# First products two units ahead of second products in the unpinned half of an attention and two-mixer kernel

## The chip, the cores and the metric

The kernel runs on one core of one Trainium2 chip. The metric is the device time of one execution in microseconds (us). The kernel before took 886.29 us, the median of 3 runs (883.88 to 888.55).

## The reference, cut to what matters

Three blocks follow one another on 4 sequences of 576 tokens and 512 features. The first is an attention (a coarse one over means of 4 tokens, plus a local one over 7 neighbours). The second and third are mixers; all weights are float32.

```
x  = attention(q, k, v)                                   # (4, 576, 512)
xn = (x - mean) / sqrt(var + 1e-6) * g_ln
x  = x + max(xn @ w_ch1, 0) @ w_ch2                       # w_ch1 512x2048, w_ch2 2048x512
h  = max(x^T @ w_tok1, 0) @ w_tok2                        # over tokens: 576x256, 256x576
u  = x + h^T
out = u + max(u @ w_ch1', 0) @ w_ch2'                     # w_ch1' 512x1536, w_ch2' 1536x512
```

## The kernel before, in words

The 2304 tokens are 18 tiles of 128, two tiles to a chunk: 9 chunks for the first channel mixer (chunks 0 to 8) and 9 for the second (chunks 9 to 17). A **unit** is one chunk with 128 hidden features. A chunk has 16 units in the first mixer and 12 in the second, 252 units in all (`seq`, lines 858 to 860). Chunk 7 begins with unit 112, chunk 9 with unit 144, and units 144 to 155 are chunk 9.

A unit has four steps.

- `g1` (line 868), the first products: 12 matmuls of 256 columns into a PSUM bank `h`. Each float32 operand is kept as two fp32r halves, high and low, and three of the four combinations are multiplied (`PASSES`: high-high, high-low, low-high), for each of four slices of the 512 features.
- `relu` (line 882): ScalarE (ACT) writes the high half of the hidden tile `ht` from `h`.
- `low` (line 886): VectorE (DVE) writes the low half of `ht` from `h` and the high half.
- `g2` (line 892), the second products: 6 matmuls of 512 columns from `ht` and the second weight into two accumulators `acc`. Four of the six need the high half of `ht` alone, the other two its low half.

Two buffers each hold `h`, `ht` and `acc` (`bufs=2`, lines 208, 210 and 211).

Up to unit 111 the order of everything is a table written out by hand (`STEPS`), pinned with `manual_schedule`. **Behind unit 112** the kernel only traces its instructions in a loop over units (lines 1205 to 1214, in the diff below): first products of a later unit, the background steps that `put` has hung on this unit (`mid`), second products of this unit, a chunk's end, and more background steps (`bg`). The Tile framework then makes each engine's order from this by priority and its own model of time. So an engine's order can differ from the traced one, and the place of a background step moves when the loop changes.

The background steps that the prediction touches:

- **Weights of the second mixer**: 24 pieces of 512 KB. The queue of SyncE (SP) issues a load into a staging buffer `st` (line 298, two buffers). Three DVE steps turn a piece from float64 into float32 (`cv`, lines 257, 262, 267). ACT writes the high half (`w`, line 272) and DVE the low half (line 275).
- **Token tiles**: each of the 4 sequences has five tiles for the token mixer. `xs_load` (line 961) loads a tile from DRAM into `xr`, of which there is one buffer (lines 962 and 970, or 968 for the fifth tile, in two pieces). `xs_split` (line 973): ACT writes the high half of `xs` (line 976), GpSimd (POOL) the low half (line 977). `tok1` (line 983): six matmuls (line 992) into banks `k`. After a sequence's fifth tile `tok_relu` (line 997) makes `r` on ACT and DVE, and `tok2` (line 1012) multiplies it by the second token weight (line 1023).
- **Turning of `u`** for the next chunk: `xt_turn`, 32 small DMAs a chunk on the SP queue (line 818).

```
    def xs_load(b, n):
        t = tok["pool"].tile([128, DM], F32, tag="xr", name="xr", bufs=1)
...
    def xs_split(b, n):
        r = xs[b, n]
        t = tok["pool"].tile([128, 2, DM], F32R, tag="xs", name="xs", bufs=2)
        nc.scalar.activation(out=t[:, 0], in_=r, func=ACTF.Copy)
        nc.gpsimd.tensor_tensor(out=t[:, 1], in0=r, in1=f32(t[:, 0]), op=ALU.subtract)
```

Of the kernel before, what the change touches and what calls it, by code (L numbers as in the profile page):

```python
# [170 lines left out]
UNITS = 112  # L171
# [26 lines left out]
def block_kernel(ctx: ExitStack, tc: tile.TileContext, qk, vw, vh, vg, g_ln, wa, t1, t2, wb, band, near, lv, edge, out):  # L198
# [693 lines left out]
    def g2(i):  # L892
        c, m = seq[i]
        w = wunit(c, m)
        t = hT.pop(i)
        last = m == nunits(c) - 1
        for j in range(CT):
            if m == 0:
                acc[c, j] = psg("k" if c == 1 else "acc")
            for n, (a, e) in enumerate(PASSES):  # L900
                nc.tensor.matmul(  # L901
                    out=acc[c, j], lhsT=t[:, a, j * 128:(j + 1) * 128], rhs=w[:, 1, e, :],
                    start=(m == 0 and n == 0), stop=(last and n == 2),
                )
# [16 lines left out]
    def chunk_end(i):  # L921
        c, m = seq[i]
        if m == nunits(c) - 1:
            with tc.high_priority(offset=HP2):
                for j in range(CT):
                    evac(i, j)
                    store(i, j)
# [103 lines left out]
    NSEQ = len(seq)  # L1031
# [171 lines left out]
    put_tok(3, base[NCH + 4])  # L1203

    for i in range(UNITS, NSEQ):
        if i + 1 < NSEQ:
            for f in (g1, relu, low):
                f(i + 1)
        for f in mid[i]:
            f()  # L1210
        g2(i)
        chunk_end(i)
        for f in bg[i]:
            f()
# [121 lines left out]
```

## Time and profile before

| | |
|---|---|
| median of 3 runs (range) | 886.29 us (883.88 to 888.55) |
| profiled execution: its own time | 886.56 us |
| profiled execution: span of the trace | 884.8 us |
| mean granted TensorE clock | 0.998 |
| TensorE (PE) busy | 863.8 us, 98% |
| weight loads (PEld) busy | 766.3 us, 87% |
| DVE, ACT, POOL busy | 518.4, 251.4 and 193.6 us |

A profile is one execution. Its times count from the start of the span, which is 1.8 us shorter than the execution's own time. Line numbers are those of the kernel before. PE is matmuls; a "releaser" is what ended an engine's wait.

### The profile page before, as it was taken

How to read it: one execution, taken by the hardware profiler on the slowest of the kernel's cores; microseconds unless marked ns; L12 is line 12 of the kernel's file. 1: busy time of each engine (PE TensorE's matmuls, PEld its weight loads, DVE VectorE, ACT ScalarE, POOL GpSimd, SP SyncE). 2: the span in 40 equal slices, each digit the busy share in tenths (PEclk: the TensorE clock that was granted, in tenths of full speed). 3: DMA queues.
4: the chain of work that ended last, by engine and by line, in shares of the span. 5: the costliest groups of instructions: out<-in, count | busy, mean ns of one | idle time of the engine just before them, and what ended most of it. 6: DMA issues, size and time to landing. Idle time of an engine off the chain costs nothing.

```text
span 884.8 us, 16767 instructions
## 1 busy us (share of the span) xinstructions
PE 863.8 (98%) x6418; PEld 766.3 (87%) x6418; DVE 518.4 (59%) x1114; ACT 251.4 (28%) x713; POOL 193.6 (22%) x197
## 2 busy tenths in 40 slices
PE   7999999999999999999999999989999999999998
PEld 6888899887989999989999887879898898999997
DVE  5999999999998776832222779863213232222221
ACT  5665535354322111322111233222121111111111
POOL 7731323566873510111000000110010000000000
PEclk9999999999999999999999999999999999999999
DMA  9747776578662522532111356632222121121100
GB/s 280 193 151 225 225 237 199 148 199 224 168 150 72 139 49 60 175 92 89 36 37 48 107 155 178 193 115 53 52 56 46 29 67 35 17 45 23 31 24 24
DMA packets 126752, 98.39 MB, mean 111 GB/s; under 512 B 78744, under 2 KB 104376, under 8 KB 126672
## 3 DMA queue, kind: packets, MB, share of 16 engines
q1 hardware_dynamic: 126672, 97.31, 39.4%
q8 instruction: 51, 0.84, 0.4%
q14 instruction: 29, 0.24, 0.1%
HBM read 72.87 MB, written 16.53 MB: 101 GB/s over the span
## 4 chain that ended last, share of the span: by engine, by line
PE 66%; DVE 19%; DMA 8%; SPq 3%; issue 2%; POOL 1%; ACT 1%; DVEq 0%; ACTq 0%; POOLq 0%
PE h L875 30%; PE acc L901 27%; DMA xr<-x_scr 3%; DMA st<-in_wb_dram 3%; SPq L818 3%; PE k L901 2%; DVE cv L267 2%; PE g L1023 2%; DVE ht L888 1%; DVE cv L262 1%; DVE lp L718 1%; DVE la L726 1%; DVE cv L257 1%; PE k L992 1%; DMA up_scr<-od 1%
## 5 line engine op out<-in xcount | busy, mean ns | idle before, releaser
L875 PEld LDWEIGHTS h<-xt,w 128*128 128x128 f32 x3024 | 394.2, 191 | 22.9 <-DVE ht L888 2.1
L875 PE MATMUL h<-xt,w 128*128 128x256 f32 x3024 | 404.8, 284 | 1.4 <-DVE ht L888 1.3
L901 PE MATMUL acc<-w,ht 128*128 128x512 f32 x1416 | 367.7, 395 | 3.0 <-DVE ht L888 2.4
L901 PEld LDWEIGHTS acc<-w,ht 128*128 128x128 f32 x1416 | 253.5, 189 | 52.3 <-DVE ht L888 4.6
L888 DVE SCALAR_TENSOR_TENSOR ht<-h,ht 128x256 fp32r<-128x256 f32 x252 | 105.6, 419 | 273.4 <-ACT ht L884 273.0
L884 ACT ACTIVATE ht<-h 128x256 fp32r<-128x256 f32 x252 | 96.7, 384 | 439.0 <-PE h L875 355.8
L977 POOL TENSOR_TENSOR xs<-xr,xs 128x512 fp32r<-128x512 f32 x20 | 26.5, 1323 | 293.3 <-ACT xs L976 293.3
L272 ACT ACTIVATE w<-cv 128x512 fp32r<-128x512 f32 x56 | 35.5, 635 | 66.6 <-DVE cv L267 66.5
L684 POOL TENSOR_TENSOR lp<-lqk 128x576 f32<-128x576 f32 x28 | 40.4, 1444 | 43.2 <-DVE ls L690 31.5
L275 DVE TENSOR_TENSOR w<-cv,w 128x512 fp32r<-128x512 f32 x56 | 42.8, 767 | 4.3 <-ACT w L272 4.1
L267 DVE SCALAR_TENSOR_TENSOR cv<-st,cv 128x512 int32<-128x512 int32 (+4 forms) x63 | 44.2, 703 | 0.4
L655 POOL TENSOR_TENSOR x<-x,et 128x256 f32<-128x256 f32 (+2 forms) x40 | 32.0, 820 | 50.6 <-DMA et<-loc_scr 40.0
L262 DVE SCALAR_TENSOR_TENSOR cv<-st,cv 128x512 int32<-128x512 int32 (+4 forms) x63 | 41.5, 659 | 0.4
L257 DVE TENSOR_SCALAR cv<-st 128x512 int32<-128x512 int32 (+4 forms) x63 | 27.3, 433 | 15.2 <-DMA st<-in_wb_dram 10.5
L455 POOL TENSOR_TENSOR vg<-vg 72x256 f32<-72x256 f32 x39 | 31.4, 806 | 18.3 <-DMA vg<-in_vg_dram 15.3
L992 PE MATMUL k<-xs,t1w 128*128 128x512 f32 (+1 forms) x120 | 32.1, 406 | 2.6 <-ACT xs L976 1.9
L1023 PE MATMUL g<-r,t2w 128*128 128x512 f32 x120 | 34.0, 394 | 0.0
L830 ACT ACTIVATE xt<-xt 128x512 fp32r<-128x512 f32 x30 | 18.9, 631 | 34.6 <-DMA xt<-xc 31.2
L835 DVE TENSOR_TENSOR xt<-xt 128x512 fp32r<-128x512 f32 x30 | 24.1, 803 | 7.3 <-ACT xt L830 7.0
L901 PE MATMUL k<-w,ht 128*128 128x512 f32 x96 | 26.0, 403 | 0.1
L992 PEld LDWEIGHTS k<-xs,t1w 128*128 128x128 f32 (+1 forms) x120 | 19.2, 188 | 7.9 <-ACT xs L976 2.8
L1023 PEld LDWEIGHTS g<-r,t2w 128*128 128x128 f32 x120 | 20.9, 189 | 3.0
(189 smaller groups left out, 656.4 us busy)
## 6 DMA issues: line engine op xcount, KB each, us to landing
st<-in_wa_dram SPq DMA_DIRECT2D x28, 512.0 KB
st<-in_wb_dram SPq DMA_DIRECT2D x24, 512.0 KB
xt<-xc SPq DMA_DIRECT2D x480, 16.0 KB
qk<-in_qk_dram SPq DMA_DIRECT2D x13, 581.0 KB
x_scr<-x SPq DMA_DIRECT2D x18, 256.0 KB
x<-x_scr SPq DMA_DIRECT2D x9, 512.0 KB
out_dram<-x SPq DMA_DIRECT2D x18, 256.0 KB
xr<-x_scr SPq DMA_DIRECT2D x16, 256.0 KB
```

The costliest lines, as they stand in the source:

```text
L257: return nc.vector.tensor_scalar(out=f, in0=h, scalar1=3, scalar2=0x3FFFFFFF, op0=ALU.logical_shift_left, op1=ALU.bitwise_and)
L262: nc.vector.scalar_tensor_tensor(out=f, in0=h, scalar=-0x40000000, in1=f, op0=ALU.bitwise_and, op1=ALU.bitwise_or)
L267: nc.vector.scalar_tensor_tensor(out=f, in0=l, scalar=29, in1=f, op0=ALU.logical_shift_right, op1=ALU.bitwise_or)
L272: nc.scalar.activation(out=hi, in_=f.bitcast(F32), func=ACTF.Copy)
L275: nc.vector.tensor_tensor(out=lo, in0=f.bitcast(F32), in1=f32(hi), op=ALU.subtract)
L684: nc.gpsimd.tensor_tensor(out=t["pr"], in0=t["qk"][:, :VQ], in1=t["qk"][:, VQ + D * o:VQ + D * o + VQ], op=ALU.mult)
L875: nc.tensor.matmul(out=hp[:, :CN], lhsT=w[:, 0, a, kk * 128:(kk + 1) * 128], rhs=xT[c][:, kk, e, :], start=(n == 0), stop=(n == 3 * KD - 1),)
L884: nc.scalar.activation(out=t[:, 0], in_=hps[i][:, :CN], func=ACTF.Relu)
L888: nc.vector.scalar_tensor_tensor(out=t[:, 1], in0=hp[:, :CN], scalar=0.0, in1=f32(t[:, 0]), op0=ALU.max, op1=ALU.subtract)
L901: nc.tensor.matmul(out=acc[c, j], lhsT=t[:, a, j * 128:(j + 1) * 128], rhs=w[:, 1, e, :], start=(m == 0 and n == 0), stop=(last and n == 2),)
L992: nc.tensor.matmul(out=rps[b, m], lhsT=tokw["t1"][rows, a, n, m * 128:(m + 1) * 128], rhs=t[rows, e, :], start=(n == 0 and i == 0), stop=( ...
L1023: nc.tensor.matmul(out=ps, lhsT=tokw["t2"][:, a, m, o:o + 128], rhs=r_t[b][:, m, e, :], start=(i == 0), stop=(i == len(ops) - 1),)
```

## The change

In the loop behind unit 112 the first products, `relu` and `low` that are traced ahead of unit i's second products are those of unit i+2 and no longer those of unit i+1. The first turn of the loop traces two units to get there.

```diff
     for i in range(UNITS, NSEQ):
-        if i + 1 < NSEQ:
+        for k in range(i + 1 if i == UNITS else i + 2, min(i + 3, NSEQ)):
             for f in (g1, relu, low):
-                f(i + 1)
+                f(k)
         for f in mid[i]:
             f()
         g2(i)
```

The instructions and their sizes are the same; their order differs on all engines. Names carry numbers here; tiles made late in the kernel have a number 16 higher after the change (`xs_7864` is the `xs_7848` of before).

**TensorE, in the middle of chunk 12.** Each `h` is one unit's first products, each `ht` one unit's second products; `xt` is the chunk's turned input, `w` weights. Before:

```order
L875 MATMUL h_8143<-xt_7712,w_6599 128x256 x12
L1023 MATMUL g_8781<-r_7919,t2w_5752 128x512 x3
L901 MATMUL acc_8068<-w_6531,ht_8097 128x512 x2
L901 MATMUL acc_8072<-w_6531,ht_8097 128x512
L901 MATMUL acc_8068<-w_6531,ht_8097 128x512
L901 MATMUL acc_8072<-w_6531,ht_8097 128x512 x2
L875 MATMUL h_8165<-xt_7712,w_6650 128x256 x12
```

After:

```order
L875 MATMUL h_8159<-xt_7728,w_6666 128x256 x12
L901 MATMUL acc_8084<-w_6547,ht_8073 128x512
L901 MATMUL acc_8088<-w_6547,ht_8073 128x512
L901 MATMUL acc_8084<-w_6615,ht_8113 128x512 x2
L901 MATMUL acc_8088<-w_6615,ht_8113 128x512 x2
L875 MATMUL h_8181<-xt_7728,w_6714 128x256 x12
```

Before, the six second products of a unit stand together between two units' first products. After, the four that need only the high half stand ahead of the first products of the unit two later, and the two that need the low half stand behind them.

**TensorE, around the fourth and fifth token tile of the third sequence** (here without numbers, so that equal rows merge). Line 992 is `tok1`, line 1023 `tok2`. Before, the first row is the fourth tile, the next six-matmul row of line 992 the fifth; the rows of line 875 between them are units 155 (in two pieces) and 156, those of line 901 unit 154:

```order
L992 MATMUL k<-xs,t1w 128x512 x6
L875 MATMUL h<-xt,w 128x256 x2
L901 MATMUL acc<-w,ht 128x512 x4
L875 MATMUL h<-xt,w 128x256 x10
L901 MATMUL acc<-w,ht 128x512 x2
L875 MATMUL h<-xt,w 128x256 x12
L992 MATMUL k<-xs,t1w 128x512 x6
L901 MATMUL acc<-w,ht 128x512 x6
L875 MATMUL h<-xt,w 128x256 x24
```

After, the first row is the last four matmuls of the fourth tile, the row of ten is unit 154, the rows of line 901 are units 153, 154 and 155, and the row of 24 is units 155 and 156:

```order
L992 MATMUL k<-xs,t1w 128x512 x4
L875 MATMUL h<-xt,w 128x256 x10
L901 MATMUL acc<-w,ht 128x512 x6
L992 MATMUL k<-xs,t1w 128x512 x6
L875 MATMUL h<-xt,w 128x256 x24
L901 MATMUL acc<-w,ht 128x512 x6
L1023 MATMUL g<-r,t2w 128x512 x2
L901 MATMUL acc<-w,ht 128x512 x4
L1023 MATMUL g<-r,t2w 128x512 x8
```

The fifth tile's products have moved ahead of the first products of units 155 and 156 and the second products of unit 154. Counted from unit 113 on, 528 first and 258 second products stand ahead of them before and 504 and 252 after, with 54 matmuls of line 992 and 60 of line 1023 both times.

**SP and ACT, at the same tiles.** `xr_7785`, `xr_7818` and `xr_7851` are the loads of the third, fourth and fifth tile of that sequence, `xr_8397` that of the next sequence's first; `st` are weight pieces. The SP queue before:

```order
L970 DMA xr_7785<-x2_scr5_123 128x512
L298 DMA st_6882<-in_wb_dram 128x1024
L298 DMA st_6915<-in_wb_dram 128x1024
L970 DMA xr_7818<-x2_scr6_124 128x512
L298 DMA st_6923<-in_wb_dram 128x1024
L968 DMA xr_7851<-x2_scr6_124 64x512 x2
L970 DMA xr_8397<-x2_scr7_125 128x512
```

The SP queue after:

```order
L970 DMA xr_7801<-x2_scr5_123 128x512
L298 DMA st_6890<-in_wb_dram 128x1024
L970 DMA xr_7834<-x2_scr6_124 128x512
L298 DMA st_6898<-in_wb_dram 128x1024
L298 DMA st_6931<-in_wb_dram 128x1024
L968 DMA xr_7867<-x2_scr6_124 64x512 x2
L298 DMA st_6939<-in_wb_dram 128x1024
L970 DMA xr_8413<-x2_scr7_125 128x512
```

ACT after, from the fifth tile's copy on (`w_6963` is the weight of unit 155, `ht_7272` the `relu` of unit 155):

```order
L976 ACTIVATE xs_7898<-xr_7867 128x512
L272 ACTIVATE w_6924<-cv_6933 128x512
L272 ACTIVATE w_6963<-cv_6964 128x512
L884 ACTIVATE ht_7248<-h_7235 128x256
L976 ACTIVATE xs_8466<-xr_8413 128x512
L272 ACTIVATE w_6963<-cv_6970 128x512
L1001 ACTIVATE r_7935<-k_7790 128x512
L1001 ACTIVATE r_7935<-k_7791 128x512
L884 ACTIVATE ht_7272<-h_7259 128x256
L976 ACTIVATE xs_8519<-xr_8469 128x512
```

On SP the fourth tile's load (`xr_7818`, after `xr_7834`) has moved ahead of two weight pieces, so that only one is left between it and the third tile's, and the fifth tile's ahead of one. On ACT the copy of the next sequence's first tile now stands ahead of the last weight piece and of the `relu` of unit 155; before, that piece and that `relu` stood ahead of the copy.

## Rows read from the trace of the kernel before

**Rows 1.** The page, part 1: engine, busy us and share of the span.

```profile
PE 863.8 (98%) x6418; PEld 766.3 (87%) x6418; DVE 518.4 (59%) x1114; ACT 251.4 (28%) x713; POOL 193.6 (22%) x197
```

**Rows 2.** Busy time by stretch of 20 us: stretch, length, each engine, clock, DMA.

```profile
560.00:580.00 20.00, 18.50 (x100) 14.90 (x99) 15.55 (x27) 4.92 (x10) 3.17 (x2) 1.00 0.61 195
580.00:600.00 20.00, 18.27 (x106) 15.17 (x107) 12.01 (x20) 6.02 (x13) 3.94 (x3) 1.00 0.32 91
600.00:620.00 20.00, 20.00 (x124) 17.91 (x123) 6.79 (x13) 4.36 (x10) 1.29 (x1) 1.00 0.24 61
...
780.00:800.00 20.00, 20.00 (x129) 18.18 (x128) 5.58 (x12) 3.32 (x8) 0.00 (x0) 1.00 0.23 50
```

**Rows 3.** PE's waits from 430 us on: line, releaser, us in total, times, longest.

```profile
PE k L992 <- ACT xs L976: 1.9, 2, 1.6
PE acc L901 <- DVE ht L888: 0.8, 3, 0.4
PE k L992 <- POOL xs L977: 0.7, 1, 0.7
PE acc L901 <- ACT ht L884: 0.6, 1, 0.6
PE h L875 <- DVE ht L888: 0.2, 1, 0.2
```

**Rows 4.** The chain that ended last, one unit behind 750 us: start, us, what.

```profile
752.41 1.43 PE h L875 x12
753.85 1.39 PE acc L901 x6
```

**Rows 5.** The page, part 5: DVE's and ACT's step of a unit, mean ns.

```profile
L888 DVE SCALAR_TENSOR_TENSOR ht<-h,ht 128x256 fp32r<-128x256 f32 x252 | 105.6, 419 | 273.4 <-ACT ht L884 273.0
L884 ACT ACTIVATE ht<-h 128x256 fp32r<-128x256 f32 x252 | 96.7, 384 | 439.0 <-PE h L875 355.8
```

**Rows 6.** PE in order of time: start, us, what [idle before and releaser].

```profile
580.79 0.73 PE L992 MATMUL k<-xs,t1w 128*128 128x512 f32 x2 [1.61 <-ACT xs L976]
582.22 1.19 PE L992 MATMUL k<-xs,t1w 128*128 128x512 f32 x4 [0.69 <-POOL xs L977]
...
587.89 0.97 PE L992 MATMUL k<-xs,t1w 64*128 64x512 f32 x6
...
593.64 1.55 PE L1023 MATMUL g<-r,t2w 128*128 128x512 f32 x6
```

**Rows 7.** SP's DMA issues in order of time: start, us, what.

```profile
567.97 0.33 SPq L970 DMA_DIRECT2D xr<-x_scr  x1
571.12 4.58 SPq L298 DMA_DIRECT2D st<-in_wb_dram  x2
575.80 0.37 SPq L970 DMA_DIRECT2D xr<-x_scr  x1
580.45 0.33 SPq L298 DMA_DIRECT2D st<-in_wb_dram  x1
582.19 1.31 SPq L968 DMA_DIRECT2D xr<-x_scr  x2
587.90 0.33 SPq L970 DMA_DIRECT2D xr<-x_scr  x1
```

**Rows 8.** POOL in order of time: the low halves of the third and fifth tile.

```profile
573.30 1.49 POOL L977 TENSOR_TENSOR xs<-xr,xs 128x512 fp32r<-128x512 f32 x1 [5.36 <-ACT xs L976]
...
586.58 1.30 POOL L977 TENSOR_TENSOR xs<-xr,xs 128x512 fp32r<-128x512 f32 x1 [4.41 <-ACT xs L976]
```

**Rows 9.** The chain of waits: time from issue to landing of two tile loads.

```profile
575.80 4.20 DMA xr<-x_scr
...
583.02 2.75 DMA xr<-x_scr
```

**Rows 10.** ACT in order of time: fifth tile, next sequence's first tile, then `r`.

```profile
585.87 0.63 ACT L976 ACTIVATE xs<-xr 128x512 fp32r<-128x512 f32 x1 [2.22 <-DMA xr<-x_scr]
586.40 0.62 ACT L272 ACTIVATE w<-cv 128x512 fp32r<-128x512 f32 x1
...
590.69 0.63 ACT L976 ACTIVATE xs<-xr 128x512 fp32r<-128x512 f32 x1 [3.40 <-DMA xr<-x_scr]
...
591.49 1.08 ACT L1001 ACTIVATE r<-k 128x512 fp32r<-128x512 f32 x2
```

## The prediction

> **What bounds the kernel now.** I read the page's shares first, then the stretches of 20 us, then PE's own waits, and last the order of time on PE, SP, POOL and ACT where those waits lie. PE is busy for 98% of the span and nothing else comes near [rows 1]. From 600 us on PE has no idle time at all, while between 560 and 600 us it loses 1.50 and 1.73 us [rows 2]. The granted clock is 1.00 in all these stretches, the upper level of 2.4 GHz, and the change leaves PE as busy, so the clock is no term. From 430 us on, which is about where unit 113 begins, PE waits 1.9 + 0.8 + 0.7 + 0.6 + 0.2 = 4.2 us in all [rows 3]. That is the most that a better order can win back by its waits: 0.47% of 886 us. Of the 4.2 us, 2.6 are waits of the token products for a tile's halves and 1.6 are waits for `relu` and `low`.
>
> Work does not change: a unit still costs 1.43 us of first and 1.39 us of second products [rows 4], back to back. So the time can only move through waits.
>
> [...]
>
> **Part 1: the steady order, nothing.** A longer lead is meant to give `relu` and `low` more time. Before, unit i's `relu` may begin when its first products end, and its result is needed after the second products of unit i-1 and the first of unit i+1: 1.39 + 1.43 = 2.82 us [rows 4]. After, the first products lead by one unit more, but `ht` still has two buffers: `relu` of unit i waits until the last two second products of unit i-2 have read theirs. By the new order there lie between these and the four second products of unit i that need its result the other four of unit i-1, the first products of unit i+1 and two of unit i-1: again 2.82 us. The two steps need 0.38 + 0.42 us [rows 5]. Behind 600 us both orders are covered by some 2 us, and where 2.82 us did not do (the 1.6 us of waits), the same time will not do better. I carry these 1.6 us over unchanged; if all of them went, the time would be 1.6 us lower, and I keep that for the range.
>
> The split of the second products into four and two costs nothing that rows of before show: neighbours on PE are back to back there whatever their kind.
>
> **Part 2: the fifth token tile of the third sequence, +4.26 us.** The same products of `xs` now stand ahead of 24 first and 6 second products that came before them. PE reaches them earlier by 2 x 1.43 + 1.39 = 4.25 us [rows 4] of work (4.26 with unrounded rows), and this work then lies behind them, on the path to the end. Before, PE came to them at 587.89 without a wait [rows 6]. POOL finished this tile's low half at 586.58 + 1.30 = 587.88 us [rows 8]. The third matmul is the first that needs it; at 0.97 / 6 = 0.16 us each it began at about 588.2, so 0.3 us were in hand. If the tile were ready when it is now, the loss would be 4.26 - 0.3 = **+4.0 us**.
>
> **Part 3: its load comes sooner, -2.5 us.** `xr` has one buffer, so the loads form a chain: load, ACT copy, POOL subtraction, next load. The issues stand at 567.97, 575.80, 582.19 and 587.90 [rows 7], steps of 7.83, 6.39 and 5.71 us. In the first step POOL was done with the third tile at 573.30 + 1.49 = 574.79 [rows 8], but SP issued at 575.80: it stood behind two weight pieces that took it 4.58 us, from 571.12 on. That is 1.01 us, and the new SP order leaves one piece there. The fourth tile's load then took 4.20 us to land, beside a weight piece issued just ahead of it; the fifth's took 2.75 [rows 9]. With that piece now issued behind it I expect a landing like the fifth's: 1.45 us. Together 2.46, say 2.5 us. The bounds: nothing, if the transfers share the DMA engines as before; and 7.83 + 6.39 - 2 x 5.71 = 2.8 us, if both steps shrink to the shortest seen. I take a value near the upper bound because its two pieces are each a row. The fourth tile, which made PE wait 1.61 + 0.69 us [rows 6], is moved by less work (one unit, 2.82 us) and gains the same load time, so its wait stays about what it is.
>
> **Part 4: `relu` behind a tile copy on ACT, +0.2 us.** On ACT the copy of the next sequence's first tile now stands ahead of the last weight piece, `r` and the `relu` of unit 155. Before, it ran 590.69 - 585.87 = 4.82 us after the fifth tile's copy [rows 10]. With the fifth tile's copy 2.5 us earlier, at 583.4, it would run at 588.2 to 588.8; then the weight's half 0.6, `r` 1.08 [rows 10] and `relu` 0.4 us: 590.9. PE has the fifth tile's low half at 587.88 - 2.5 = 585.4, needs 4 x 0.16 for the rest and 4.26 for the units 155, 156 and 154, and two products of line 1023 at 1.55 / 6 = 0.26 each [rows 6]: 590.8. The two meet, with 0.1 to 0.3 us lost. This is 0 at best; every microsecond by which that copy is later comes onto PE whole.
>
> **The sum.** 886.56 (the profiled execution's own time, 0.27 above the median of the runs) + 4.0 - 2.5 + 0.2 = 888.3 us, +1.7 us or 0.2%. PE's idle time from 430 us on would go from 4.2 to about 5.9 us. About 0.5% (4.4 us) is what a measurement of this kernel can tell from no change: so forecast **no difference**. With the bounds of part 3 and the waits of part 1 this case alone runs from 886.4 (2.8 won, 1.6 us of waits gone) to 890.8 (part 3 nothing).
>
> **Rivals.**
>
> *The queues give it all back (slower).* Place: ACT and SP at 575 to 595 us. The last four weight pieces now stand on SP behind tile loads that wait for POOL, so they come later, and on ACT the copy of the next sequence's tile holds the last weight piece and the `relu` of unit 155. If part 3 gives nothing and that copy comes 2 us later than reckoned, PE pays 4.0 + 2.0 = 6 us: 892.6 us. It decides from the point where the copy ends after 590.5 with the fifth tile ready no sooner than 587. For it: SP did hold a load for 1.01 us in the old order, loads took between 2.75 and 4.20 us [rows 9], and the slack on ACT is a few tenths. Against it: the new order lets the tile loads ahead, not behind. The Trainium skill, "PSUM — Partial Sum Buffer", section "Engine vs sequencer instructions", calls the queues of ScalarE, VectorE and GpSimd strict FIFO. By that rule a late copy delays everything traced behind it; this case's rows agree in that ACT sat 3.40 us for that load with a `relu` behind it [rows 10].
>
> *The lead hides the waits (faster).* If the tile loads come 2.8 us sooner and the merged order elsewhere lets `relu` and `low` be in time, most of the 4.2 us goes: 882.4 us. Against it: part 1 shows that two buffers of `ht` leave the same 2.82 us, and the tile products have moved towards their data, not away.
>
> *It does nothing.* Two `h` and two `ht` buffers allow no true lead of two; if the loads gain what the order asks for, parts 2 to 4 cancel: 886.6 us.
>
> **How the numbers follow.** Forecast (887 to 890.7) 0.50, nothing 0.18, slower rival 0.24, faster rival 0.08. The range reaches from 883.2 to 892.8: it holds the forecast and the case of nothing, most of the slower rival and part of the faster. Faster by over 0.5% (below 881.9) needs all 4.2 us: 0.06. Slower by over 0.5% (above 890.7) is the slower rival and a little of the forecast's end: 0.26. The rest is 0.68.
>
> **What would show it.** Right: PE's idle from 430 us on at 5 to 7 us, nearly all of it before 600 us; the wait of line 992 for ACT and POOL grown from 2.6 to about 4 us, with a new wait at the fifth tile; the fourth and fifth tile's loads issued 1 to 3 us sooner against the third's; no idle behind 610 us. Part 1 is wrong if waits for line 888 vanish or grow by over 1 us. Part 3 is wrong if the steps between the tile loads stay at 7.8 and 6.4 us. Part 4 is wrong if PE waits over 1 us for the `relu` of unit 155. The prediction as a whole fails if PE shows new gaps behind 610 us, where I give both orders 2 us of cover, or if the later sequences' tiles, which have also moved forward, make it wait.

## The result and the profile after

The changed kernel takes 891.68 us (median of 8 runs, 888.10 to 909.94), the kernel before 886.01 us in the same comparison (8 runs). The ratio is **1.0051, 95% interval [1.0035, 1.0067]**: about 4.5 us slower. The forecast was 888.3 us, +1.7 us, and it was called no difference. The sign is right and the time lies in the range, near its upper end, but the loss is over twice what the sum said and clear of nothing, and the sections below show that most of it came by another way.

The longest run is the profiled one: it ran at a lowered clock in its first 60 us, where nothing is changed, so the ratio leaves it out, and the trace shown most is that of the first experiment, the same program once more with an empty line ahead of it: its line numbers are one higher.

The repetition's page, part 1 (span, then busy us and share):

```profile
span 892.8 us, 16768 instructions
...
PE 869.6 (97%) x6418; PEld 769.4 (86%) x6418; DVE 516.2 (58%) x1114; ACT 251.9 (28%) x713; POOL 194.2 (22%) x197
```

The work is that of [rows 1]. From the start of unit 113's first products (434.27 us here, 432.28 before) to the end of the span it is 892.8 - 434.27 = 458.5 us, against 884.8 - 432.28 = 452.5 before. **6.0 us are to be found behind unit 113.** TensorE's waits from 430 us on, in the repetition (line, releaser, us in total, times, longest), which answer to [rows 3]:

```profile
PE k L993 <- ACT xs L977: 5.2, 3, 2.9
PE g L1024 <- DVE r L1003: 0.9, 1, 0.9
PE k L993 <- POOL xs L978: 0.7, 1, 0.7
```

The same view of the first profile of the changed kernel:

```profile
PE k L992 <- ACT xs L976: 5.6, 5, 1.9
PE k L992 <- POOL xs L977: 1.2, 2, 0.8
PE h L875 <- DVE ht L888: 0.8, 1, 0.8
PE g L1023 <- DVE r L1002: 0.6, 1, 0.6
```

That is 6.8 and 8.2 us, for 4.2 before. The waits for `relu` and `low`, 1.6 us in [rows 3], have shrunk to 0 and 0.8; the token products' waits have grown from 2.6 to 5.9 and 6.8. The steps of a unit have kept their length (the repetition's page, part 5; [rows 5] before):

```profile
L889 DVE SCALAR_TENSOR_TENSOR ht<-h,ht 128x256 fp32r<-128x256 f32 x252 | 105.6, 419 | 271.8 <-ACT ht L885 271.0
L885 ACT ACTIVATE ht<-h 128x256 fp32r<-128x256 f32 x252 | 96.8, 385 | 442.8 <-PE acc L902 302.7
```

ACT's wait ahead of `relu` used to end with the first products (line 875); now it mostly ends with second products (line 902), which free the `ht` buffer. That is what part 1 said of two buffers.

Where the waits lie, in PE's order of time (start, us, what, idle before and releaser):

```profile
528.25 0.73 PE L993 MATMUL k<-xs,t1w 128*128 128x512 f32 x2 [1.28 <-ACT xs L977]
...
535.49 0.50 PE L993 MATMUL k<-xs,t1w 64*128 64x512 f32 x2 [1.00 <-ACT xs L977]
...
544.17 1.67 PE L1024 MATMUL g<-r,t2w 128*128 128x512 f32 x6 [0.95 <-DVE r L1003]
...
572.63 1.22 PE L993 MATMUL k<-xs,t1w 128*128 128x512 f32 x2 [2.90 <-ACT xs L977]
...
590.70 0.73 PE L993 MATMUL k<-xs,t1w 64*128 64x512 f32 x4 [0.70 <-POOL xs L978]
```

The longest is not at the fourth or fifth tile of the third sequence, where [rows 6] had 1.61 + 0.69 us and where the prediction looked, but at its **second** tile. Two more stand at the last tiles of the second sequence. The fifth tile of the third waits 0.70 us here, 1.42 + 0.85 us in the first profile. To the second tile TensorE came no sooner than before: at 572.63 - 2.90 - 434.27 = 135.5 us behind unit 113, for 135.6 before. It was the tile that came later. And the long wait has a second price. Stretches of 2 us around it (stretch, length, PE, PEld, DVE, ACT, POOL busy, granted clock, DMA share, GB/s):

```profile
568.00:570.00 2.00, 1.73 (x8) 1.08 (x7) 0.92 (x3) 0.42 (x1) 0.00 (x0) 1.00 0.57 162
570.00:572.00 2.00, 0.00 (x0) 0.00 (x0) 2.00 (x4) 0.25 (x2) 0.00 (x0) 0.92 0.95 313
572.00:574.00 2.00, 1.37 (x3) 1.16 (x4) 1.11 (x2) 1.65 (x4) 1.28 (x1) 0.50 0.69 236
574.00:576.00 2.00, 2.00 (x6) 1.53 (x5) 2.00 (x5) 0.63 (x1) 0.00 (x0) 0.50 0.37 120
576.00:578.00 2.00, 2.00 (x8) 1.71 (x8) 1.66 (x4) 0.10 (x1) 0.00 (x0) 0.50 0.76 290
578.00:580.00 2.00, 2.00 (x14) 1.87 (x14) 0.92 (x1) 0.67 (x2) 1.29 (x1) 0.88 0.02 8
```

The granted clock fell to 0.50, the lower level of 1.2 GHz, while TensorE still waited (0.92 in the stretch from 570 us on, in which it did nothing), and it came back in the stretch from 578 us on. The low clock costs something only where TensorE works, so from 572.63 us on: 1.37 x 0.50 + 2 x (0.50 + 0.50 + 0.12) = 2.9 us. With 6.8 - 4.2 = 2.6 us more of waits that is 5.5 of the 6.0 us; where the other 0.5 us went is not shown.

In the first profile, 908.1 - 449.45 = 458.65 us behind unit 113 for 452.52, it is 8.2 - 4.2 = 4.0 us of waits and 1.7 us of clock, 5.7 of 6.1 us. There the dip follows the two waits at the fifth tile; PE in order of time:

```profile
603.67 0.50 PE L992 MATMUL k<-xs,t1w 64*128 64x512 f32 x2 [1.42 <-ACT xs L976]
605.02 0.73 PE L992 MATMUL k<-xs,t1w 64*128 64x512 f32 x4 [0.85 <-POOL xs L977]
605.68 4.88 PE L875 MATMUL h<-xt,w 128*128 128x256 f32 x24
```

The last row is two units' first products, 2 x 1.43 = 2.86 us by [rows 4]. The stretch they stand in, by the same profile's windows:

```profile
600.00:610.00 10.00, 7.73 (x41) 6.26 (x40) 7.66 (x12) 4.30 (x9) 2.55 (x2) 0.83 0.33 104
```

**Were the loads sooner?** The chain of waits of the repetition, from the second tile's load to the fifth's (start, us, what), answers to [rows 7, 9]:

```profile
567.16 4.71 DMA xr<-x_scr
...
571.95 0.64 ACT xs L977
...
573.96 3.86 DMA xr<-x_scr
...
579.93 2.50 DMA xr<-x_scr
...
585.08 3.15 DMA xr<-x_scr
```

The third tile's issue is at 573.96, the fourth's at 579.93 and the fifth's at 584.54 (its row in the chain, from 585.08 on, is that of its second piece): steps of 5.97 and 4.61 us for 7.83 and 6.39 before. So the two steps together became 3.6 us shorter, more than the 2.5 reckoned. But the chain starts late. Counted from unit 113, the third tile's load stood at 567.97 - 432.28 = 135.7 us before and stands at 573.96 - 434.27 = 139.7 now. All that was won went into catching up with a chain that begins 4.0 us later, and the second tile had no time to catch up.

### The profile page after: what moved, and what is told of

It reads as the page before. It is cut to its first block, busy times and chain, and to the rows that moved or that the text cites. A ratio compares the mean times of both kernels' runs of the same rounds, so it can differ in the third digit from the quotient of the medians.

```text
span 908.1 us, 16768 instructions
## 1 busy us (share of the span) xinstructions
PE 881.4 (97%) x6418; PEld 778.8 (86%) x6418; DVE 523.0 (58%) x1114; ACT 251.2 (28%) x713; POOL 188.0 (21%) x197
## 4 chain that ended last, share of the span: by engine, by line
PE 70%; DVE 17%; DMA 7%; ACT 2%; issue 1%; SPq 1%; POOL 1%; DVEq 0%; ACTq 0%; POOLq 0%
PE h L875 31%; PE acc L901 28%; DMA xr<-x_scr 2%; PE g L1023 2%; PE k L992 2%; DVE cv L267 1%; DVE la L726 1%; DMA st<-in_wb_dram 1%; DVE ht L888 1%; DVE cv L262 1%; PE k L901 1%; DVE lp L718 1%; DVE xc L770 1%; SPq L818 1%; DVE cv L257 1%
## 5 line engine op out<-in xcount | busy, mean ns | idle before, releaser
L275 DVE TENSOR_TENSOR w<-cv,w 128x512 fp32r<-128x512 f32 x56 | 44.8, 804 | 4.9 <-ACT w L272 4.7
```

Of the source, the lines that this page charges most:

```text
L275: nc.vector.tensor_tensor(out=lo, in0=f.bitcast(F32), in1=f32(hi), op=ALU.subtract)
```

## The experiments

In the diffs below `...` marks lines left out. All twelve runs, in order of the ratio to the kernel before (its median was 887.0 to 887.4 us in these comparisons). "First weight" is the first high half that ACT writes of the second mixer's weights (line 272), in us from the start of unit 113's first products:

| kernel | ratio, 95% interval | first weight |
|---|---|---|
| before, conversions one unit earlier (before_sp1) | 0.9989 [0.9969, 1.0010] | 53.9 |
| lead of two for units 142 to 156 (lead_b) | 1.0002 [0.9987, 1.0018] | 62.4 |
| change, conversions one unit earlier (after_sp1) | 1.0004 [0.9980, 1.0027] | 54.6 |
| change, conversions not pinned (after_free) | 1.0005 [0.9986, 1.0024] | 52.6 |
| lead of two from unit 157 on (lead_late) | 1.0017 [0.9998, 1.0037] | 62.4 |
| lead of two for units 112 to 140 (lead_a) | 1.0042 [1.0025, 1.0060] | 67.1 |
| before, a second `xr` buffer (before_xr2) | 1.0052 [1.0034, 1.0070] | 62.4 |
| the change again (after_again) | 1.0057 [1.0026, 1.0087] | 67.1 |
| before, conversions one unit later (before_late) | 1.0059 [1.0039, 1.0080] | 62.6 |
| change, a second `xr` buffer (after_xr2) | 1.0065 [1.0049, 1.0081] | 67.1 |
| lead of two for units 112 to 156 (lead_early) | 1.0069 [1.0045, 1.0093] | 67.1 |
| change, token products held back (after_hold) | 1.0102 [1.0075, 1.0130] | 67.1 |

### Which units cost it, and is it the tiles' place?

The first theory (A) was the prediction's own: TensorE reaches the token tiles before their loads have come. Its rival (B) was a loss spread over the steady order.

*The change again:*

> The changed kernel as it is, for a second trace. Both theories expect 890 us, 1.004 to 1.006 of before. Theory A (the token tiles of the second and third sequence are multiplied ahead of the arrival of their loads) expects PE's waits from unit 113 on at 7 to 9 us, of which 5 to 7 are waits of line 992 for ACT and POOL. Theory B (the loss is spread: the steady order with two buffers of ht, and stretches at the lower clock) expects line 992 at about the 2.6 us of before, and the rest as waits of lines 875 and 901 or as stretches with a granted clock under 0.95 behind unit 113.

It gave 1.0057 [1.0026, 1.0087], and the trace above. Its waits, 5.9 us on line 992 of 6.8 in all, are about what theory A named; the stretch at the lower clock is what B named.

*The lead for units up to 156 only, and from 157 on only:*

```diff
+    done = [UNITS]
     for i in range(UNITS, NSEQ):
-        if i + 1 < NSEQ:
+        while done[0] < min(i + (2 if i < 157 else 1), NSEQ - 1):
+            done[0] += 1
             for f in (g1, relu, low):
-                f(i + 1)
+                f(done[0])
```

The second kernel has `i >= 157` in place of `i < 157`.

> Lead of two units for units 112 to 156 alone, of one unit from 157 on. The token tiles of the second and third sequence stand in PE's order as in the changed kernel. Theory A: all of the loss stays, 1.004 to 1.006 of before. Theory B: about a third of the loss, 1.001 to 1.002, since a third of the units have the new order.

> Lead of one unit for units 112 to 156, of two units from 157 on. PE's order is that of before up to the fifth tile of the third sequence. Theory A: no loss, 0.999 to 1.001. Theory B: two thirds of the loss, 1.003 to 1.004.

1.0069 and 1.0017. The first has all of the loss, where theory B had a third of it: B falls. The second cannot be told from nothing, though its interval reaches to 1.0037; 95 units run there with the new lead, and the fourth sequence's fifth tile stands behind 684 first products, for 816 before, without a wait. So most of the loss, if not all, comes from units 112 to 156. `lead_early` has the same long wait at the same tile, and one more at a second product of the token mixer (PE in order of time):

```profile
568.58 0.74 PE L992 MATMUL k<-xs,t1w 128*128 128x512 f32 x2 [2.54 <-ACT xs L976]
...
620.04 0.95 PE L1023 MATMUL g<-r,t2w 128*128 128x512 f32 x3 [2.04 <-DVE x L1028]
```

*The tiles held at their old place:* the token products of the third and fourth sequence are issued behind the same unit's first products as before.

```diff
+    HOLD = {(2, 0): 152, (2, 1): 152, (2, 2): 153, (2, 3): 154, (2, 4): 156,
+            (3, 0): 165, (3, 1): 169, (3, 2): 171, (3, 3): 176, (3, 4): 180}
...
+    def tok1_held(b, n):
+        if (b, n) in HOLD:
+            with tc.issue_after(g1_end[HOLD[b, n]].ins):
+                tok1(b, n)
+        else:
+            tok1(b, n)
...
-            put(u + 2 + n, tok1, b, n)
+            put(u + 2 + n, tok1_held, b, n)
```

> The changed kernel, with the token products of the third and fourth sequence queued on PE behind the same units' first products as in the kernel before; only those of the second sequence stay where the change puts them. Theory A: most of the loss goes, 1.000 to 1.002, and line 992 waits 2 to 4 us. Theory B: 1.004 to 1.006, as the changed kernel.

1.0102, worse than the change. PE in order of time:

```profile
584.43 0.50 PE L878 MATMUL h<-xt,w 128*128 128x256 f32 x2 [1.25 <-ACT w L272]
...
599.52 1.32 PE L905 MATMUL acc<-w,ht 128*128 128x512 f32 x4 [3.04 <-ACT ht L888]
```

The tiles wait only 2.5 us now, all of it for ACT and all of it at the second sequence's last two tiles, which are not held; the held ones do not wait. But a weight and a `relu` are late in their stead. Theory A in its simple form falls: with the third sequence's tiles at their old place the loss does not go. (The hold also bends the scheduler's order elsewhere, so its size says little.)

### Two places, or something that starts early?

Theory C was that the loss has two separate places: the last tiles of the second sequence, and the second tile of the third. Its rival was that each unit with the new lead in this crowded stretch adds its share. The lead was given to two groups of units, by the loop edit above with `i < 141` and with `142 <= i < 157`.

> Lead of two units for units 112 to 140 alone, of one from 141 on, so that chunk 8 ends (unit 143) in the order of before. The fourth and fifth tile of the second sequence stand as in the changed kernel, the third sequence's tiles about as before. Theory C (the loss has two places: about 2 us at the second sequence's last tiles and their r, where the fifth tile's load is cut in two around a weight piece; about 3 us at the third sequence's second tile, whose load stands on SP behind stores of chunk 8 that now come a unit later) expects 1.001 to 1.003 and no wait over 1 us at the third sequence's second tile. The rival (each unit with the lead of two loses its part wherever DVE and the DMA queue are crowded) expects 1.003 to 1.005, since units 130 to 140 are half of the crowded stretch.

> Lead of two units from 142 to 156 alone. Up to unit 142 all stands as before; chunk 8 ends with the new order. Theory C: 1.002 to 1.004, the wait at the third sequence's second tile is 2 us or more and the second sequence's last tiles wait under 0.5 us. The rival: 1.003 to 1.005 too, but spread over waits of the units.

1.0042 and 1.0002. The second is below both of its expectations. It does not test the fifth tile: 528 first and 258 second products stand ahead of that tile there, as before. But its second tile stands as early as in the change, behind 468 first products (480 before), and TensorE does not wait for it; its load is issued 565.24 - 434.71 = 130.5 us behind unit 113, for 132.9 in the change. The first run lies where the rival had it, above theory C's range. So neither stands for both runs. The first run ends its lead at unit 140, and yet its longest waits lie where units 152 to 155 run; PE in order of time:

```profile
570.17 1.19 PE L901 MATMUL acc<-w,ht 128*128 128x512 f32 x4 [1.21 <-ACT ht L884]
...
573.22 0.73 PE L901 MATMUL acc<-w,ht 128*128 128x512 f32 x2 [1.38 <-DVE ht L888]
...
587.09 0.50 PE L875 MATMUL h<-xt,w 128*128 128x256 f32 x2 [1.02 <-ACT w L272]
```

The first products of unit 141 run at about 524 us there. So a lead that is over makes TensorE wait some 45 to 60 us later, when the order of units is again the old one. This points to something that is carried along on another engine's queue.

*A second `xr` buffer,* in memory that is free there, once in the changed kernel and once in the kernel before:

```diff
-        t = tok["pool"].tile([128, DM], F32, tag="xr", name="xr", bufs=1)
+        t = grow if (b + n) % 2 else tok["pool"].tile([128, DM], F32, tag="xr", name="xr", bufs=1)
```

> The changed kernel with a second buffer for the token tiles' loads: every other tile is loaded into the memory of g_ln, which nothing reads any more by then. The loads then wait for no POOL subtraction of the tile before. Theory C: the waits of line 992 shrink below 3 us and the time to 0.998 to 1.002 of before. The rival: 1.004 to 1.006, as without it.

> The kernel before with the same second buffer for the token tiles' loads. Both theories: the 2.6 us of waits of line 992 go in part, 0.997 to 1.000 of before. It is the control for the run above: if it gains as much as the changed kernel does, the single buffer is a cost of its own and not what the lead of two pays for.

1.0065 and 1.0052: it helps neither, and that the kernel before would lose by it no theory had expected. In the change the waits for tiles shrank to 0.6 us, as theory C had said, but 3.3 us of waits for weights came and the time stayed. In the kernel before it took the tiles' long waits away and put one wait for a weight of chunk 9 in their place:

```profile
588.07 0.80 PE L875 MATMUL h<-xt,w 128*128 128x256 f32 x2 [3.21 <-ACT w L272]
```

SP's one queue issues both, and here what the tiles won the weights lost. The waits of `before_xr2` add up to 4.2 us, as before; the low clock around this wait took 2.4 us. The rest of the loss is not shown: behind unit 113 this profile is only 1.8 us longer than that of before.

### The weight stream of the second mixer

The last column of the table gave theory D. Where the conversions hang on the units of before, ACT begins the first weight 67.1 us behind unit 113 in every kernel with the lead over units 112 to 140, and at 62.4 in those without it. Here is why. In the kernel before, DVE in order of time:

```profile
491.42 0.42 DVE L888 SCALAR_TENSOR_TENSOR ht<-h,ht 128x256 fp32r<-128x256 f32 x1 [0.57 <-ACT ht L884]
...
491.83 0.42 DVE L257 TENSOR_SCALAR cv<-st 128x512 int32<-128x512 int32 x1
```

In the repetition of the change:

```profile
493.41 0.42 DVE L889 SCALAR_TENSOR_TENSOR ht<-h,ht 128x256 fp32r<-128x256 f32 x1 [2.64 <-ACT ht L885]
...
497.17 0.42 DVE L889 SCALAR_TENSOR_TENSOR ht<-h,ht 128x256 fp32r<-128x256 f32 x1 [0.38 <-ACT ht L885]
...
497.77 0.42 DVE L258 TENSOR_SCALAR cv<-st 128x512 int32<-128x512 int32 x1
```

The `low` at 491.42 and that at 493.41 are both 59.1 us behind unit 113. Before, the first conversion of the second mixer's weights follows 0.4 us behind it, at 59.6. After the change **one more `low`** stands ahead of it, and it runs at 63.5. The conversions are hung on units 131 and following, and their first step is pinned to the place in which it is traced:

```
    def split_unit(i, part, pinned=True):
        first, *rest = split_steps(i, part)
        ins = first()
        if pinned:
            tc.keep_in_program_order(ins)
...
    for m in range(UB):
        put(bw + 3.5 + m, w_split, NPC)
```

With the lead of two, the `low` of unit i+2 and no longer of unit i+1 has been traced ahead of what hangs on unit i. The conversion frees the staging buffer, and so the next piece's load is late too. The chain of waits of the repetition:

```profile
493.41 0.42 DVE ht L889
...
495.44 0.59 SPq L819
...
501.15 0.60 SPq L819
501.86 3.77 DMA st<-in_wb_dram
```

SP's issues there, in order of time, with the eight turning DMAs in one row:

```profile
495.44 6.31 SPq L819 DMA_DIRECT2D xt<-xc  x8
```

Before, the chain has `495.16 3.65 DMA st<-in_wb_dram` here: the reload was issued 62.9 us behind unit 113, behind one of chunk 9's 32 small turning DMAs. Now it stands on SP behind eight of them, at 67.6. From there on the stream's weights are 2 to 8 us later on ACT, with SP's turning DMAs and tile loads between its pieces: the second tile's load at 561.87 - 432.28 = 129.6 before and 567.16 - 434.27 = 132.9 now, its copy on ACT at 133.3 and 137.7, the last weight copy at 586.40 - 432.28 = 154.1 [rows 10] and 593.90 - 434.27 = 159.6. The Trainium skill, "PSUM — Partial Sum Buffer", section "Engine vs sequencer instructions", calls VectorE's queue strict FIFO. The trace agrees: the loads of both staging buffers were issued at 378.65 and 403.74 us, and DVE idled 2.64 us ahead of the `low` at 493.41 without taking up the conversion behind it.

Theory D: this late stream is the loss. Its rival: the lead itself, whatever the stream's start. They part where the conversions are moved back by one unit under the change, and moved on by one unit without it.

```diff
     for m in range(UB):
-        put(bw + 3.5 + m, w_split, NPC)
+        put(bw + 2.5 + m, w_split, NPC)
```

> The change with each pinned weight conversion of the second mixer hung one unit earlier (2.5 in place of 3.5). Theory D (the lead of two puts the pinned conversions behind a low that runs one unit later, so the second mixer's weight stream and with it SP's queue start 4.5 us late): 1.000 to 1.003; first weight copy on ACT no later than 62.5 us behind the start of unit 113 (before 62.4, the change 67.0), and the second token tile of the third sequence waits under 1 us on TensorE. Rival (the lead itself, whatever the stream's start): 1.004 to 1.007, that tile still 2 us or more.

1.0004 [0.9980, 1.0027]: the loss is gone, with the lead of two in place for all units behind 112. TensorE's waits from 430 us on:

```profile
PE acc L901 <- ACT ht L884: 0.6, 2, 0.4
PE k L992 <- POOL xs L977: 0.3, 1, 0.3
```

0.9 us in all, the least of any run here, and no dip of the clock behind 430 us while TensorE works. The first weight is at 54.6, the second tile's copy at 132.3. One more thing moved with this edit: the fifth tile of the third sequence stands behind 528 first and 258 second products again, as before.

*The kernel before, one unit later* (4.5 in place of 3.5):

> The kernel before with each pinned conversion of the second mixer one unit later (4.5). Theory D: 1.002 to 1.006, first weight copy 64.5 us or later behind unit 113, and a wait of TensorE of over 1.5 us on a token tile of the third sequence or on a weight. Rival: 0.999 to 1.001.

1.0059 [1.0039, 1.0080]: the loss is there without the lead. The marks that theory D named came only in part. TensorE's waits from 430 us on:

```profile
PE k L992 <- POOL xs L977: 1.6, 2, 0.9
PE k L992 <- ACT xs L976: 1.3, 1, 1.3
PE acc L901 <- DVE ht L888: 1.2, 1, 1.2
PE h L875 <- DVE w L275: 0.5, 1, 0.5
PE acc L901 <- DVE w L275: 0.4, 1, 0.4
PE acc L901 <- ACT ht L884: 0.3, 1, 0.3
```

No single wait is over 1.5 us, and the first weight is at 62.6, hardly later than before. The lateness builds up behind it: the last weight copy is at 160.6 us for 154.1 before, and the fifth tile of the third sequence stands behind 504 first and 252 second products, as in the change. The 5.3 us of waits are 1.1 more than before, and the clock gave up 1.7 us in 580 to 600. From unit 113 on this kernel is 4.0 us longer (891.0 - 434.45 = 456.55 for 452.52); the remaining 1.2 us I could not place.

*The kernel before, one unit earlier,* and *the change with no conversion of the second mixer pinned:*

```diff
-        if pinned:
+        if pinned and i < UA:
             tc.keep_in_program_order(ins)
```

> The kernel before with each pinned conversion of the second mixer one unit earlier (2.5). Theory D: 0.997 to 1.000, first weight copy at 59.5 us or earlier, TensorE's idle time from 430 us on under the 4.2 us of before. Rival: 1.000, or slower by other transfers on SP's queue pushed back.

> The change with the second mixer's conversions not pinned at all, so the scheduler places them by its own costs. Theory D: 0.998 to 1.003, as with one unit earlier or better, weight copies no later than in the kernel before. Rival: 1.004 to 1.007.

0.9989 [0.9969, 1.0010] and 1.0005 [0.9986, 1.0024], with 2.2 and 2.9 us of waits and first weights at 53.9 and 52.6. Both times land where theory D had them. One mark of `after_free` fails: its weights are not all as early as before, since the twelfth begins at 112.2 us for 108.0. Neither is faster than the kernel before by what these runs can tell, and nor is `after_sp1`, whose profile has 3.3 us less of waits than that of before. No version was shown to beat both kernels.

What this settles: an edit of the conversions' place alone makes the loss come and go, under the new lead and without it. The place of the fifth tile does not do it: in `after_free` it stands behind 506 first and 252 second products, nearly as in the change (504 and 252), and TensorE does not wait for it, while `lead_a` and `after_hold` have it behind 528 and 258, as before, and lose.

What stays open is which part of the stream counts, and how the loss divides over late tiles and late weights: in the change the tiles wait, in `before_late` tiles, weights and `low`. The stream's start does not separate the kernels (62.6 in `before_late`, 62.4 in `before_xr2`, both with a loss), nor does its middle (`after_free`). Its end does: the last weight copy begins at 149.4 to 154.1 us behind unit 113 in the six kernels without the loss, the kernel before among them, and at 155.2 to 160.6 in the eight profiles with it. That a late end is the cause, and not one more effect, is not shown. Every one of these edits lets the scheduler reorder other things as well, and `before_xr2` shows that such a reordering can cost 0.5% by itself, with the stream's start where it was.

## Why the prediction was right or wrong

- **Sign and range: right, in part by luck.** Slower, within the range, most of the loss ahead of 600 us in the repetition, and no idle there behind 610 us beyond 0.05 us up to TensorE's last products. But "no difference" was wrong, 1.0051 with an interval clear of 1, and the largest costs in the repetition, the wait at the second tile (2.90 us) and the clock (2.9 us), were not in the sum.
- **Part 1, the steady order: half right.** The lead of two behind unit 157 costs nothing that can be told from zero (1.0017), and `relu` waits on second products, as said. But the 1.6 us of waits for `relu` and `low` were carried over unchanged and shrank to 0 and 0.8; by the prediction's own sign, that waits for line 888 vanish, this part is wrong in the repetition.
- **Parts 2 and 3, the fifth tile and its loads: the mechanism there, the balance wrong.** The new wait at the fifth tile came (1.42 + 0.85 us, or 0.70, for 4.0 - 2.5 = 1.5 reckoned), and the two steps between loads shrank by 3.6 us for 2.5 reckoned. Where the weights come sooner, the tile's early place costs nothing (`after_free`, above). **The step that failed** is the one that hung the chain of loads on an unchanged start: "If the tile were ready when it is now", with its load 2.5 us sooner. The third tile's load starts 4.0 us later; the weight stream that shares SP's queue with it starts some 20 units ahead of that tile and was moved behind one more `low`, and with that undone the loss is gone (1.0004). Of the fourth tile the text said that its wait stays about what it is: of 2.30 us nothing was left in the repetition and 0.77 us in the first profile. The waits moved to the third sequence's second tile (2.90 and 1.90 us) and the second sequence's last two, which the text did not price.
- **Part 4, `relu` of unit 155: right.** No wait of TensorE for it in either profile; "0 at best" was the value.
- **The clock, "no term": wrong.** The waits of [rows 3] had left it at 1.00. The longer ones cost 2.9 us in the repetition and 1.7 us in the first profile, about a half and over a quarter of the loss. Waits of 6.8 and 8.2 us were also more than the 5.9 of the sum.
- **The rival "the queues give it all back"** came nearest in its price (6 us) and in naming SP's queue. Its place was wrong: the lateness begins not on ACT at 575 to 595 us but on DVE and SP at 490 us.

## What to carry to other kernels

When a loop's lead is changed, everything that is hung on its units by number and pinned to its traced place moves with it: list the pinned steps of other streams first, and find what is now traced ahead of each. Here a stream began 4 us late, and TensorE's waits came 30 to 90 us behind that point, so the order around the waits does not show it; compare, from a common unit on, when each stream begins and ends. Price a long wait of TensorE at more than its length: each of the six single waits of over 2 us in these profiles (2.02 to 3.21 us) came with a dip of the granted clock that cost 1.7 to 2.9 us more.

## What the hardware did that I had not expected

The clock's price is counted here where TensorE works at 0.50, in us of work lost. The wait of 2.90 us in the repetition cost 2.9 us in this way, as much as the wait itself: the clock was at 0.50 from before its end until about 6 us behind it. The waits of 3.04 us (`after_hold`), 2.54 and 2.04 us (`lead_early`) and 2.02 us (`after_xr2`) cost 1.7 us each, that of 3.21 us (`before_xr2`) 2.4 us. Two waits close together were enough as well: 1.42 and 0.85 us in the first profile of the change, with 0.5 us of work between them, cost 1.7 us (0.83 over 10 us). A wait of 1.58 us in `after_hold` was followed by a dip that cost 1.7 us too. Yet 1.90 us in the first profile of the change, the 1.61 and 0.69 us of [rows 6] and the 1.21 and 1.38 us of `lead_a` left the clock at 1.00. So the length of the last wait alone does not say whether the clock falls.
